# Gathered expert rows transposed by DMA instead of TensorE, their weights gathered in two parts, in an attention and two-layer expert kernel

## The chip, the cores and the metric

One core of one Trainium2 chip runs the whole program. The metric is device time in microseconds (us) of one execution. Of the kernel before, three runs were timed: 1859.72, 1863.57 and 1864.79, median 1863.57 us.

## What is computed

A strided/local attention (4 batches, 8 heads, 576 positions, head size 64) gives 2304 tokens of 512 numbers. A first expert layer (8 experts, hidden size 1024) applies all experts to all tokens with Sinkhorn weights. The second expert layer, which the change touches, gives each token to one expert, 288 tokens to each:

```python
def _moe2_ref(x, w_gate, w1, w2):
    N, D = x.shape
    E = w_gate.shape[1]
    cap = N // E
    logits = x @ w_gate
    flat = logits.flatten()
    order = np.argsort(-flat)
    ...
    for idx in order:
        tok, e = (int(idx) // E, int(idx) % E)
        if assigned[tok] >= 0 or counts[e] >= cap:
            continue
        assigned[tok] = e
        counts[e] += 1
    ...
    for e in range(E):
        mask = assigned == e
        h = np.maximum(x[mask] @ w1[e], 0.0)
        out[mask] = h @ w2[e]
```

## The kernel before

Attention and the first expert layer take the first 1600 us and are not touched. They leave each token's row in DRAM as `xd`: 512 high halves and 512 low halves in fp16, and a scale, 2052 bytes in all. The weights of the second layer lie in DRAM as four tensors `wd[0..3]` (high and low halves of the first and of the second matrix), 1 MB for each expert and tensor.

The second layer is done in eight phases, one for each expert, in an order that the routing finds while the phases run (`ffn`, L1532; `ph` is the phase's number). A phase has a first matrix (8 blocks `f`, 12 matmuls each, L1549) and a second one (4 blocks `d`, 24 matmuls each, L1579). The results are turned back by TensorE (`pty`, L1522) and stored row by row (L1525) in the next phase's first matrix.

What the next phase needs comes in three ways:

- The routing (`route`, `place`) names the next expert (`wis`) and its tokens (`places`). It is a chain between TensorE and VectorE: compare (L1211), count (`pcnt`, L1217), select (L1219), `pany` (L1223) and so on, and at last `pidx` (L1394) and the list of row numbers (L1400).
- `load_w2` gathers the four weight tensors from DRAM, as soon as `wis` is known, into one of three sets of buffers (`w3`).
- `ffn_g` gathers the 288 rows as three tiles `g0` to `g2` of 96 rows each, as soon as `places` is known; this is at block `d` = 1. `ffn_x` then turns one tile: 8 transposes on TensorE into one bank `ptg` (L1469), a copy by ScalarE into `xg` (L1470), and the rows' scales `osc` on VectorE (L1471). It is called for the three tiles in the middle of `d` = 2, at the start of `d` = 3 and in the middle of `d` = 3. The first matrix of the next phase reads all 288 columns of `xg` in each matmul, so it needs all three tiles.

Phase 0 gets its `xg` in another way (`ffn_x0`), which is not changed; so there are seven turns from a phase to the next, 21 tiles in all.

The order of TensorE's work is the order in which this code is written: `drive` draws units of `ffn` and steps of the routing in turn. On the other engines a scheduler sets the order in each engine's stream, by when it expects each instruction to be ready. GpSimd (POOL) issues all the gathers and row stores, SyncE (SP) issues the plain DMAs and has none left after the last `xd` store (L1073).

Of the kernel before, what the change touches and what calls it, by code (L numbers as in the profile page):

```python
# [10 lines left out]
F16 = mybir.dt.float16  # L11
BF16 = mybir.dt.bfloat16
I32 = mybir.dt.int32
AF = mybir.ActivationFunctionType
# [4 lines left out]
N, DM, E, F = 2304, 512, 8, 1024  # L19
CAP = N // E  # L20
WIN = 32
DC = DM // 128
# [233 lines left out]
class Kernel:  # L256
# [21 lines left out]
    def bank(self, name, tag="bank"):  # L278
        tag = tag if tag in self.banks else "l1"
        return self.psum.tile([128, 512], F32, name=name, tag=tag, bufs=self.banks[tag])  # L280
# [1154 lines left out]
                t = next(routes, None)  # L1435
                self.wait = 1e9 if t is None else self.wait + t

    def load_w2(self, ph):
        for k in range(4):
            self.nc.gpsimd.indirect_dma_start(out=self.w3[ph % 3][k].rearrange("p a b -> p (a b)"), out_offset=None,  # L1440
                                              in_=self.wd[k],
                                              in_offset=bass.IndirectOffsetOnAxis(ap=self.wis[ph][:, :1], axis=0))
# [16 lines left out]
    def ffn_x(self, ph, s):  # L1459

        nc = self.nc
        M = 96
        if s == 0:
            self.fx[ph] = (self.fp.tile([128, 2 * DC, CAP], F16, name="xg"), self.fp.tile([96, 3], F32, name="osc"))
        gs = self.gs[ph]
        xg, osc = self.fx[ph]
        pt = self.bank("ptg", "l2").bitcast(F16)[:, 0:2 * DC * M].rearrange("p (k m) -> p k m", m=M)
        for k in range(2 * DC):
            nc.tensor.transpose(pt[:, k], gs[s][:, k * 128:k * 128 + 128], self.identh[:M, :M])  # L1469
        nc.scalar.activation(xg[:, :, s * M:s * M + M], pt, AF.Copy)  # L1470
        nc.vector.tensor_tensor(osc[:, s:s + 1], gs[s][:, 2 * DM:].bitcast(F32), self.places[ph][1][:M], op=OP.mult)  # L1471

    def ffn_x0(self):
# [58 lines left out]
    def ffn(self, routes):  # L1532

        nc, fp = self.nc, self.fp
        bank = lambda: self.bank("mm", "l1")[:, :CAP]
        for ph in range(E):
            w = self.w3[ph % 3]
            if ph + 1 < E:
                loaded = False
            xg = self.fx[ph][0]  # L1540
            hh = fp.tile([128, FC, CAP], F16, name="h2h")
            hl = fp.tile([128, FC, CAP], F16, name="h2l")
            for f in range(FC):
                ps = bank()
                fs = slice(f * 128, f * 128 + 128)
                k = 0
                for d in range(DC):
                    for l, r in ((w[0], d), (w[0], DC + d), (w[1], d)):
                        nc.tensor.matmul(ps, l[:, d, fs], xg[:, r], start=k == 0, stop=k == 3 * DC - 1)  # L1549
                        k += 1  # L1550
                    if d == 1:
                        yield
                r = fp.tile([128, CAP], F32, name="h2", bufs=5)
                nc.scalar.activation(r, ps, AF.Relu)  # L1554
                nc.scalar.activation(hh[:, f], r, AF.Copy)
                nc.vector.tensor_tensor(hl[:, f], r, hh[:, f], op=OP.subtract)
                yield
                if ph and 0 < f < 4:
                    self.ffn_y(ph - 1, f - 1)
                if ph + 1 < E and not loaded:  # L1560
                    if f == 5:
                        self.until_has(self.wis, ph + 1, routes)
                    if len(self.wis) > ph + 1:
                        self.load_w2(ph + 1)
                        loaded = True
            yt = self.fy[ph] = fp.tile([128, DC, CAP], F32, name="yt")
            for d in range(DC):
                if ph + 1 < E and d == 1:
                    self.until_has(self.places, ph + 1, routes)
                    if ph + 1 not in self.gs:  # L1570
                        self.ffn_g(ph + 1)
                if ph + 1 < E and d == 3:
                    self.ffn_x(ph + 1, 1)
                ps = bank()
                dsl = slice(d * 128, d * 128 + 128)
                k = 0
                for f in range(FC):
                    for l, r in ((w[2], hh), (w[3], hh), (w[2], hl)):
                        nc.tensor.matmul(ps, l[:, f, dsl], r[:, f], start=k == 0, stop=k == 3 * FC - 1)  # L1579
                        k += 1  # L1580
                    if f % 2 and f < FC - 1:
                        if ph + 1 < E and (d, f) in ((2, 5), (3, 3)):
                            self.ffn_x(ph + 1, 2 * d - 4)
                        if ph + 1 == len(self.places) < min(len(self.wis), E):
                            self.spare()
                        yield
                nc.scalar.activation(yt[:, d], ps, AF.Copy)
                yield
        for s in range(3):
            self.ffn_y(E - 1, s)  # L1590
# [239 lines left out]
```

## Time and profile before

| | |
|---|---|
| median of 3 runs | 1863.57 us |
| profiled execution, its own time | 1860.97 us |
| span of its instructions | 1859.2 us |
| TensorE (PE) busy | 1791.8 us, 96% |
| VectorE (DVE) busy | 1192.3 us, 64% |
| ScalarE (ACT) busy | 858.3 us, 46% |
| GpSimd (POOL) busy | 474.0 us, 25% |
| mean DMA rate | 124 GB/s |
| mean granted TensorE clock | 0.985 of full |

The span runs from the first to the last instruction; the rest of the profiled execution's own time lies around it. PE rows are matmuls, PEld rows weight loads that run beside them. A time in brackets behind a row is how long the engine sat idle before it and what it then waited for. Times in the rows of a timeline are from the start of the span; a matmul's row ends some 0.2 us after the next one starts, so what a piece of PE work takes is read from start to start.

### The profile page before, as it was taken

The numbers are of one execution on the slowest core, as the hardware profiler recorded it, in microseconds if no ns is written. First come the engines' busy times: TensorE is split into PE (matmuls) and PEld (weight loads), VectorE is DVE, ScalarE is ACT, GpSimd is POOL, SyncE is SP. The second block draws the span as 40 slices with busy tenths as digits, with TensorE's granted clock in tenths as the row PEclk, the third lists the DMA queues.
The fourth block names the chain that finished last, engine by engine and source line by source line (L and its number), as shares of the span: only waits on it lengthen the run. The fifth ranks groups of instructions, "written<-read, shape, count | busy, mean of one in ns | idle before, by whom it ended". The sixth has DMA issues, their size and how long they took to land. (4 is left out here: it accounts for less than half of the span.)

```text
span 1859.2 us, 31850 instructions
## 1 busy us (share of the span) xinstructions
PE 1791.8 (96%) x12296; PEld 1058.9 (57%) x12296; DVE 1192.3 (64%) x3081; ACT 858.3 (46%) x1956; POOL 474.0 (25%) x469
## 2 busy tenths in 40 slices
PE   7889998999999999999999999999999999899997
PEld 5757765555555545554555555555555444687786
DVE  6645456678766676667476575674673788767640
ACT  6545542476667757873324511565121110234343
POOL 2121203145434544433101300322000001323241
PEclk8889999999999999999999999999999999999999
DMA  7121021245655757653322323063011001445460
GB/s 249 57 71 41 26 80 46 80 176 193 205 197 200 238 180 251 222 171 144 125 70 78 107 76 113 35 229 134 35 46 51 24 23 62 161 154 179 172 233 26
DMA packets 77420, 230.48 MB, mean 124 GB/s; under 512 B 8580, under 2 KB 13260, under 8 KB 68660
## 3 DMA queue, kind: packets, MB, share of 16 engines
q1 hardware_dynamic: 69588, 185.44, 28.7%
q0 software_dynamic: 7680, 43.01, 6.4%
q8 instruction: 96, 1.57, 0.3%
q14 instruction: 56, 0.46, 0.1%
HBM read 165.47 MB, written 62.94 MB: 123 GB/s over the span
## 5 line engine op out<-in xcount | busy, mean ns | idle before, releaser
L978 PEld LDWEIGHTS <-w1s 128*128 128x128 f16 x3024 | 295.2, 98 | 203.2 <-issue 6.4
L1034 PE MATMUL l<-w2h,hh 128*128 128x512 f16 x864 | 327.7, 379 | 0.0
L1034 PE MATMUL l<-w2h,hl 128*128 128x512 f16 x864 | 327.7, 379 | 0.0
L1034 PE MATMUL l<-w2l,hh 128*128 128x512 f16 x864 | 327.7, 379 | 0.0
L586 POOL TENSOR_TENSOR m2l<-raw,m2h 128x512 f16<-128x512 f32 x184 | 214.6, 1168 | 335.2 <-ACT raw L585 286.7
L978 PE MATMUL l<-sx,w1s 128*128 128x384 f16 x1728 | 287.9, 326 | 4.5 <-ACT vV L993 2.0
L1034 PEld LDWEIGHTS <-hh 128*128 128x128 f16 x1728 | 168.4, 98 | 199.7
L978 PE MATMUL l<-xh,w1s 128*128 128x384 f16 x864 | 219.7, 326 | 0.7 <-ACT junk L1091 0.7
L936 DVE TENSOR_REDUCE wmx<-raw 128x1 f32<-128x512 f32 x240 | 152.4, 676 | 59.8 <-DMA raw<-in_moe_w_dram 54.6
L745 DVE SCALAR_TENSOR_TENSOR acc<-l,pe,acc 128x512 f32<-128x512 f32 x126 | 94.3, 748 | 139.8 <-PE l L1034 125.0
L892 POOL TENSOR_TENSOR raw<-raw 128x256 f32<-128x256 f32 x96 | 90.2, 944 | 291.1 <-DVE w1s L582 283.5
L584 ACT ACTIVATE m2h<-raw,wscale 128x512 f16<-128x512 f32 x184 | 130.9, 712 | 63.3 <-DVE iw L948 17.1
L993 ACT ACTIVATE vV<-l 128x384 f32<-128x384 f32 x144 | 67.9, 486 | 188.9 <-PE l L978 185.2
L698 ACT ACTIVATE hh<-l 128x256 f16<-128x256 f32 (+1 forms) x112 | 49.7, 447 | 223.9 <-PE l L695 223.6
L1034 PEld LDWEIGHTS <-hl 128*128 128x128 f16 x864 | 84.5, 98 | 102.0
L978 PE MATMUL l<-xl,w1s 128*128 128x384 f16 x432 | 141.0, 326 | 0.0
L585 ACT ACTIVATE raw<-raw,wscale 128x512 f32<-128x512 f32 x184 | 132.8, 722 | 6.0
L713 PE MATMUL l<-w2h,hh 128*128 128x512 f16 x288 | 109.8, 381 | 0.0
L713 PE MATMUL l<-w2h,hl 128*128 128x512 f16 x288 | 109.7, 381 | 0.0
L713 PE MATMUL l<-w2l,hh 128*128 128x512 f16 x288 | 109.7, 381 | 0.0
L1079 DVE SCALAR_TENSOR_TENSOR junk<-acc,raw 128x512 f32<-128x512 f32 x144 | 99.0, 688 | 2.0 <-DMA raw<-gt 0.2
L582 DVE SCALAR_TENSOR_TENSOR w1s<-raw,wscale,w1s 128x512 f16<-128x512 f32 x96 | 83.0, 904 | 20.2 <-ACT w1s L581 20.2
(360 smaller groups left out, 3081.2 us busy)
## 6 DMA issues: line engine op xcount, KB each, us to landing
raw<-in_moe_w_dram SPq DMA_DIRECT2D x120, 512.0 KB, 5.2
sx<-sd SPq DMA_DIRECT2D x15, 1536.0 KB, 6.8
wd<-m2h SPq DMA_DIRECT2D x64, 256.0 KB, 4.7
wd<-m2l SPq DMA_DIRECT2D x64, 256.0 KB, 3.3
kq<-in_qk_dram SPq DMA_DIRECT2D x16, 592.0 KB, 3.9
sd<-sx SPq DMA_DIRECT2D x3, 1536.0 KB, 5.1
acc<-in_moe_w_dram SPq DMA_DIRECT2D x2, 2048.0 KB, 14.0
vl<-in_vl_dram SPq DMA_DIRECT2D x4, 768.0 KB, 6.2
```

Source lines behind the costliest of these rows:

```text
L582: nc.vector.scalar_tensor_tensor(lo, raw, s, hi, op0=OP.mult, op1=OP.subtract)
L584: nc.scalar.activation(hi, raw, AF.Copy, scale=s)
L585: nc.scalar.activation(raw, raw, AF.Copy, scale=s)
L586: nc.gpsimd.tensor_tensor(lo, raw, hi, op=OP.subtract)
L713: nc.tensor.matmul(ps, l[:, f, js], r[:, f], start=k == 0, stop=k == 3 * FC - 1)
L745: self.last = [nc.vector.scalar_tensor_tensor(a, ps, pe[:, c:c + 1], a, op0=OP.mult, op1=OP.add).ins]
L892: nc.gpsimd.tensor_tensor(o, x, y, op=OP.subtract)
L936: nc.vector.tensor_reduce(mx[:, 2 * q + k:2 * q + k + 1], part(q)[:, k * 512:k * 512 + 512], axis=AX.X, op=OP.max, apply_absolute_value=True)
L978: self.nc.tensor.matmul(ps, self.w1s[:, fs, x, k, d], a[y][:, d], start=first and m == 0, stop=m == 5, skip_group_check=not first)
L993: copy = lambda o, i: nc.scalar.activation(o, i, AF.Copy)
L1034: nc.tensor.matmul(ps, l[:, f, js], r[:, f], start=k == 0, stop=k == 3 * FC - 1)
L1079: self.nc.vector.scalar_tensor_tensor(junk, self.acc[:, c], 1.0, self.wgb[:, e], op0=OP.mult, op1=OP.mult, accum_out=self.lg[:, c, e:e + 1])
```

## The change

The transposes and the copy of `ffn_x` become one transposing DMA issued by SyncE, from the gathered tile straight into `xg`. All three calls stand right behind the gather, at block `d` = 1. The weights' gather is split: tensors 0 and 1 are asked for where all four were, tensors 2 and 3 behind the row gather at `d` = 1. The line numbers after L1466 shift by 3 to 4.

```diff
-    def load_w2(self, ph):
-        for k in range(4):
+    def load_w2(self, ph, ks=range(4)):
+        for k in ks:
...
-        pt = self.bank("ptg", "l2").bitcast(F16)[:, 0:2 * DC * M].rearrange("p (k m) -> p k m", m=M)
-        for k in range(2 * DC):
-            nc.tensor.transpose(pt[:, k], gs[s][:, k * 128:k * 128 + 128], self.identh[:M, :M])
-        nc.scalar.activation(xg[:, :, s * M:s * M + M], pt, AF.Copy)
+        nc.sync.dma_start(out=xg[:, :, s * M:s * M + M], in_=gs[s][:, 0:2 * DM], transpose=True)
         nc.vector.tensor_tensor(osc[:, s:s + 1], gs[s][:, 2 * DM:].bitcast(F32), self.places[ph][1][:M], op=OP.mult)
...
-                        self.load_w2(ph + 1)
+                        self.load_w2(ph + 1, (0, 1))
                         loaded = True
...
                     if ph + 1 not in self.gs:
                         self.ffn_g(ph + 1)
-                if ph + 1 < E and d == 3:
-                    self.ffn_x(ph + 1, 1)
+                        for n in range(3):
+                            self.ffn_x(ph + 1, n)
+                    self.load_w2(ph + 1, (2, 3))
...
-                        if ph + 1 < E and (d, f) in ((2, 5), (3, 3)):
-                            self.ffn_x(ph + 1, 2 * d - 4)
```

Where the instructions stand after it, at three places of the turn from phase 1 to phase 2. On TensorE before, the first tile's transposes (tile `g_16733` is `g0`) stand between the second matrix and a count of the routing:

```order
18568 L1579 LDWEIGHTS acc
18569 L1579 MATMUL mm<-h2l,acc 128x288
18570 L1469 LDWEIGHTS g_16733
18571 L1469 MATMUL ptg<-identh,g_16733 128x96
...
18586 L1217 LDWEIGHTS sx
18587 L1217 MATMUL pcnt<-w1s,sx 128x40
```

They are gone, as are the 20 other blocks of eight; the matmuls before and the count behind now follow each other. On SyncE the stream ended with the `xd` stores; now 21 transposing DMAs follow, those of phase 1 and of phase 2 first:

```order
353 L1467 DMA_TRANSPOSE xg<-g_16189 128x8x96
354 L1467 DMA_TRANSPOSE xg<-g_16191 128x8x96
355 L1467 DMA_TRANSPOSE xg<-g_16193 128x8x96
356 L1467 DMA_TRANSPOSE xg<-g_16704 128x8x96
357 L1467 DMA_TRANSPOSE xg<-g_16706 128x8x96
358 L1467 DMA_TRANSPOSE xg<-g_16708 128x8x96
```

Nothing stands between or behind them on this engine. On GpSimd, before, in the first matrix of phase 1 (the weights for phase 2 are `wd_73` to `wd_76`, the row stores of phase 0 are `out_dram`):

```order
136 L1525 DMA out_dram<-y,raw_3216 2304x512
137 L1440 DMA w1s<-wd_73,raw_3216 128x4096
138 L1525 DMA out_dram<-y,raw_3216 2304x512
139 L1440 DMA w1s<-wd_74,raw_3216 128x4096
140 L1440 DMA w2h<-wd_75,raw_3216 128x4096
141 L1440 DMA w2l<-wd_76,raw_3216 128x4096
142 L1525 DMA out_dram<-y,raw_3216 2304x512
143 L1454 DMA g_16733<-xd,raw_3216 96x1026
```

and of the change:

```order
136 L1522 DMA out_dram<-y,raw_3216 2304x512
137 L1440 DMA w1s<-wd_73,raw_3216 128x4096
138 L1522 DMA out_dram<-y,raw_3216 2304x512
139 L1440 DMA w1s<-wd_74,raw_3216 128x4096
140 L1522 DMA out_dram<-y,raw_3216 2304x512
141 L1440 DMA w2h<-wd_75,raw_3216 128x4096
142 L1440 DMA w2l<-wd_76,raw_3216 128x4096
143 L1454 DMA g_16704<-xd,raw_3216 96x1026
```

The second two weight tensors move behind one row store, and still stand ahead of the rows' gather. In the other turns it is one to three stores.

## Rows read from the trace of the kernel before

**Rows 1.** The page: busy time, share of the span, instructions.
```profile
PE 1791.8 (96%) x12296; PEld 1058.9 (57%) x12296; DVE 1192.3 (64%) x3081; ACT 858.3 (46%) x1956; POOL 474.0 (25%) x469
```

**Rows 2.** Busy time by stretch: phase 1, from its first matmul to that of phase 2.
```profile
core 0: us, PE busy (x) PEld busy (x) DVE busy (x) ACT busy (x) POOL busy (x), PEclk, DMA share, GB/s
1640.70:1671.20 30.50, 30.21 (x367) 25.30 (x365) 22.86 (x103) 12.57 (x26) 9.78 (x10) 1.00 0.48 178
```

**Rows 3.** Groups of instructions, 1606 to 1860: what the change removes (busy, mean ns).
```profile
L1469 PE MATMUL ptg<-identh,g 96*128 96x96 f16 x168 | 10.6, 206 | 0.0
L1470 ACT ACTIVATE xg<-ptg 128x768 f16<-128x768 f16 x21 | 17.0, 810 | 30.8 <-PE ptg L1469 23.9 <-PE pany L1223 6.8
```

**Rows 4.** Timeline of PE, one block of eight transposes and its neighbours.
```profile
1665.37 0.29 PE L1579 MATMUL mm<-h2l,acc 128*128 128x288 f16 x1
1665.49 0.51 PE L1469 MATMUL ptg<-identh,g 96*128 96x96 f16 x8
1665.84 0.62 PE L1217 MATMUL pcnt<-w1s,sx 128*128 128x40 bf16 x18
```

**Rows 5.** Timeline, turn to phase 2: row numbers ready, last gather, last scale, `pany`.
```profile
1660.30 0.14 DVE L1400 CAST raw<-raw 96x1 int32<-96x1 f32 x1
...
1663.29 0.92 POOL L1454 DMA_INDIRECT g<-xd,raw  x1 [0.30 <-DVE w1s L1219]
...
1666.59 0.16 DVE L1471 TENSOR_TENSOR osc<-g,raw 96x1 f32<-96x1 f32 x1 [0.99 <-DMA g<-xd,raw]
...
1667.03 0.18 PE L1223 MATMUL pany<-w1s,first 128*128 128x40 bf16 x1
```

**Rows 6.** The three scales of the turns to phases 1 to 6: first and last start.
```profile
L1471 DVE TENSOR_TENSOR osc<-g,raw x3: 145/147/150, 1633.2 to 1635.6; 96x1 f32<-96x1 f32 x3
...
L1471 DVE TENSOR_TENSOR osc<-g,raw x3: 148/155/156, 1664.0 to 1666.6; 96x1 f32<-96x1 f32 x3
...
L1471 DVE TENSOR_TENSOR osc<-g,raw x3: 145/146/155, 1696.6 to 1697.8; 96x1 f32<-96x1 f32 x3
...
L1471 DVE TENSOR_TENSOR osc<-g,raw x3: 154/155/156, 1727.2 to 1729.0; 96x1 f32<-96x1 f32 x3
...
L1471 DVE TENSOR_TENSOR osc<-g,raw x3: 154/155/156, 1759.0 to 1760.0; 96x1 f32<-96x1 f32 x3
...
L1471 DVE TENSOR_TENSOR osc<-g,raw x3: 155/155/226, 1788.6 to 1790.1; 96x1 f32<-96x1 f32 x3
```

**Rows 7.** Timeline of PE: first matmuls of phases 1 to 7.
```profile
1640.69 1.51 PE L1549 MATMUL mm<-xg,acc 128*128 128x288 f16 x11
...
1671.16 0.90 PE L1549 MATMUL mm<-xg,w1s 128*128 128x288 f16 x6
...
1704.44 0.90 PE L1549 MATMUL mm<-xg,xh 128*128 128x288 f16 x6
...
1735.78 1.39 PE L1549 MATMUL mm<-xg,acc 128*128 128x288 f16 x10
...
1767.55 0.90 PE L1549 MATMUL mm<-xg,w1s 128*128 128x288 f16 x6
...
1795.77 1.51 PE L1549 MATMUL mm<-xg,xh 128*128 128x288 f16 x11
...
1821.63 3.10 PE L1549 MATMUL mm<-xg,acc 128*128 128x288 f16 x24
```

**Rows 8.** SyncE's `xd` stores of 256.5 KB, 1595 to 1610: issue (ns), time to landing.
```profile
L1073 SPq DMA_DIRECT2D xd<-w1s x2: 319/319/319, 1600.3 to 1604.2; - x2
...
DMA to landing us min/median/max: 2.6/2.6/2.6
```

**Rows 9.** The rows' gathers `g` (21 of 192 KB), 1606 to 1860: time to landing.
```profile
DMA to landing us min/median/max: 3.1/4.2/10.2
```

**Rows 10.** PE's waits, 1595 to 1860: us in total, times, longest.
```profile
PE pcnt L1217 <- DVE w1s L1211: 3.6, 4, 2.4
PE pany L1223 <- DVE w1s L1219: 3.3, 4, 1.6
```

## Prediction

> **What bounds the kernel now.** I read the page first, then the busy time by stretch, then the timeline of one turn between phases, then TensorE's waits. The page shows TensorE busy for 96% of the span and no other engine above 64% [rows 1]. The stretch of phase 1 says the same of the place that the change touches: 30.21 of 30.50 us busy at full clock, with the DMA engines half idle [rows 2]. So in the eight phases a microsecond taken from TensorE is a microsecond of the kernel, unless TensorE then waits for something else. The reader is to see two possible somethings. One is the routing's chain through VectorE: TensorE already waits for it 8 times, 6.9 us in all [rows 10]. The other is new: the first matmul of a phase needs all three transposed tiles, and these will come by DMA.
>
> **What is removed.** 168 transposes on TensorE [rows 3], 21 blocks of eight. The group's mean of 206 ns is not the price, since the instructions overlap; from start to start a block takes 1665.84 - 1665.49 = 0.35 us [rows 4]. 21 x 0.35 = 7.35 us of TensorE. The 21 copies on ScalarE, 17.0 us [rows 3], are worth nothing: ScalarE is busy 12.57 of 30.5 us in the phase [rows 2], and no wait of TensorE names it beside the two for VectorE that matter.
>
> **What of the 7.35 us is lost at once.** A block that stands between two steps of the routing also gave VectorE time. In the turn to phase 2 VectorE sat in the last `osc` until the rows had landed at 1666.59, and `pany` on TensorE followed at 1667.03 [rows 5]. That chain doesn't move with the block ahead of it, so this block's 0.35 us turns into a wait. I count two such blocks in all, 0.7 us. The bounds are none and the 15 blocks of the turns to phases 1 to 5, where the routing still runs: 5.25 us. I take a value near the low end because TensorE has only 8 waits of this kind in some 60 steps of the routing.
>
> **What is added.** 21 DMAs of 96 x 1024 fp16 numbers, 192 KB each. On SyncE they stand alone, behind its last `xd` store at 1604.2 [rows 8], so nothing is queued behind a transfer that waits for its rows but the next transfer. They occupy no compute engine. What matters is when the third one lands against when TensorE wants it. The row numbers, the gathers and the scales keep their places, so the rows land as before. The start of the last `osc` bounds this landing: in the turn to phase 2 it waited for just that [rows 5]. Without the three blocks TensorE wants `xg` 1.05 us sooner than the first matmul of the next phase shows [rows 7]. That leaves, from the third landing to the need:
>
> - to phase 1: 1640.69 - 1.05 - 1635.6 = 4.0 us
> - to phase 2: 1671.16 - 1.05 - 1666.6 = 3.5 us
> - to phase 3: 5.6; to phase 4: 5.7; to phase 5: 6.5; to phase 6: 4.6 us [rows 6, 7]
>
> In the turn to phase 7 the first matmul stands at 1821.63 and the routing has long ended; I count no wait there.
>
> **The price of a transposing DMA** is in no row. The nearest below is SyncE's store of 256.5 KB, issued in 0.32 us and landed in 2.6 us [rows 8]. The nearest above is the slowest gather of the same 192 KB tiles, 10.2 us; their median is 4.2 us [rows 9]. I take 2.6 us: same queue, like size, and in most turns the weights' traffic is over by then (DMA share 0.48 over the phase [rows 2]), while the 10.2 us belongs to a gather that queued behind weights. A transfer is issued before the one ahead has landed, as the stores are, so the third lands 2.6 us after its rows, inside the 3.5 us of the tightest turn. The wait is then 0.
>
> Here the Trainium skill speaks with two voices. "Advanced Engine Details and Errata", section "X-Bar Transpose (TRN2)", says that transposing DMAs are as fast as regular ones; by it the sum stays as it is. "VectorE: DVE Perf Modes", section "The three transpose paths", speaks against the change: it gives 390 ns to TensorE and 1309 ns to the DMA for one 128x128 block. Counted so, as an estimate, a tile of eight blocks costs 10.5 us and the six turns would wait about 149 us. No row here transposes by DMA; of TensorE's price the rows show far less, 0.35 us for eight blocks of 96 rows [rows 4].
>
> **The weights in two parts.** No work is added: 4 gathers before, 4 after. On GpSimd's stream the second two move behind one to three row stores and still stand ahead of the rows' gather, so the rows queue behind the same bytes. Each store or gather occupies GpSimd for about a microsecond [rows 5], so the second two start 1 to 4 us later. They are first read in the second matrix of the next phase, more than 15 us on: nothing. What the words say of it, two parts, hardly happens in the order of the instructions.
>
> **The sum.** -7.35 + 0.7 + 0 = -6.6 us. Against the profiled execution's own time, 1860.97, that is 1854.4. That execution lies 2.6 us under the median of the runs, so against the median 1863.57 it is 1857.0 us, 0.35% less. A measurement of this kernel can tell about 0.3%, 5.6 us, from no change; the forecast lies just beyond.
>
> **Rivals.**
>
> 1. *The transfers run one after another, at 2.6 us each.* Then the third ends 7.8 us after the first rows landed. From there to the need the six turns leave 6.4, 6.1, 6.8, 7.5, 7.5 and 6.1 us [rows 6, 7], 40.4 in all; the waits add up to 18 x 2.6 - 40.4 = 6.4 us and eat the gain: 1863.4. For it: three transfers of one queue within 1 to 3 us. Against it: the stores' 0.32 us of issue.
>
> 2. *The other side: a transposing transfer is slow, and TensorE stands at the first matmul of each phase.* One mechanism, in the six turns: transfers in turn at T each make waits of 18 T - 40.4 us. It decides from T = 2.61, where the waits equal the gain of 6.6. At 4.2 us, the median of the gathers [rows 9], the waits are 35.2 and the time is 1863.57 + 35.2 - 6.6 = 1892.2. For it: a transposing write comes in smaller pieces than any store shown, and the turn to phase 2 has only 3.5 us of room. Against it: in these turns the DMA engines have little else to do.
>
> 3. *The same at the upper end, 10.2 us a transfer* [rows 9]: 183.6 - 40.4 = 143.2 us of waits, 2000.2 us, leaving out the turn to phase 7. It is nearly what the rule of the skill's "VectorE: DVE Perf Modes" on the three transpose paths would give. Against it: such a gather shared the engines with 4 MB of weights, and that is so in the last turns alone.
>
> 4. *The routing becomes the bound.* All 15 blocks of the first five turns turn into waits for VectorE: -7.35 + 5.25 = -2.1, 1861.5. For it: VectorE is busy 22.86 of 30.5 us in the phase [rows 2]. Against it: the few waits [rows 10].
>
> **How the numbers follow.** Forecast (third transfer in time): 0.48, of which 0.33 end over 0.3% faster and 0.15 within, since 6.6 us lies so near to 5.6. Rival 1: 0.14 (0.02 faster, 0.08 same, 0.04 slower). Rival 2: 0.22, slower. Rival 3: 0.08, slower. Rival 4: 0.08 (0.01 faster, 0.07 same). Together: faster 0.36, same 0.30, slower 0.34. The predicted time is the forecast's, 1857.0. The range begins at 1855.0, where no block is lost and the runs fall a little lower, and reaches to 1892, rival 2 at the gathers' median. Outside lie rival 3, the upper part of rival 2 (0.08) and a little at the low end (0.04). The forecast's own range is 1855 to 1860.
>
> **What would show it.** Right: no group `ptg`; TensorE busy some 10 us less by the page's count; the transposing DMAs landing about 2.6 us after issue; the first matmul of each phase without a wait; the turn to phase 2 about 1 us shorter in the busy time by stretch. Rival 1 or 2: the wait view names the first L1546 matmuls behind the DMA of `xg`, the longest in the turns to phases 1, 2 and 6, and landings of the three tiles a constant step apart. Rival 4: more and longer waits at `pcnt` and `pany`. What would make the prediction wrong is above all the price of the transfer, the one number that no row carries.

## The result, and the profile after

The change takes **1886.3 us** (median of 4 runs, 1883.77 to 1891.35), the kernel before 1864.18 us (median of 4 runs beside it, 1859.72 to 1867.39). The ratio is 1.0126, 95% interval 1.0107 to 1.0144: 22 us slower by the medians and some 23.5 us by the ratio. The forecast was 6.6 us faster. The profiled execution of the change took 1883.77 us with a span of 1882.1 us, against 1860.97 and 1859.2.

The page's busy line, which answers to [rows 1]: 168 transposes fewer on TensorE and 21 copies fewer on ScalarE, as the diff says, but TensorE's busy time has not fallen: it reads 1798.1 us against 1791.8.

```profile
PE 1798.1 (96%) x12128; PEld 1057.6 (56%) x12128; DVE 1191.7 (63%) x3081; ACT 841.8 (45%) x1935; POOL 473.9 (25%) x469
```

The first matmuls of the phases, from PE's timeline (answering to [rows 7]; brackets at the end of a row hold the idle time ahead and its releaser):

```profile
1645.23 0.65 PE L1546 MATMUL mm<-xg,acc 128*128 128x288 f16 x4
...
1675.09 0.78 PE L1546 MATMUL mm<-xg,w1s 128*128 128x288 f16 x5
...
1706.34 0.65 PE L1546 MATMUL mm<-xg,xh 128*128 128x288 f16 x4
...
1739.54 0.65 PE L1546 MATMUL mm<-xg,acc 128*128 128x288 f16 x4
...
1770.41 0.65 PE L1546 MATMUL mm<-xg,w1s 128*128 128x288 f16 x4
...
1817.96 4.30 PE L1546 MATMUL mm<-xg,xh 128*128 128x288 f16 x20 [15.30 <-DMA acc<-wd,raw]
...
1844.47 0.78 PE L1546 MATMUL mm<-xg,acc 128*128 128x288 f16 x5
```

In six of the seven turns TensorE doesn't wait at the phase's first matmul. In the turn to phase 6 it stands for 15.30 us. That is most of what this execution loses: the phases are 17.0 us longer in sum (from the first matmul of phase 0, 1612.83, to the end: 269.3 us against 252.3). The other 5.9 us of the profile's difference lie ahead of phase 0, which starts at 1612.83 here and at 1606.94 before. Another profiled execution of the kernel before, taken later, starts phase 0 at 1613.38, so this part is taken as scatter between executions.

The stretches of phase 1 and phase 5 (answering to [rows 2]; same columns) show the good and the bad turn:

```profile
1645.23:1675.09 29.86, 29.45 (x343) 24.30 (x340) 22.82 (x103) 10.18 (x23) 9.91 (x10) 1.00 0.61 201
1770.42:1817.96 47.54, 29.13 (x246) 23.08 (x244) 15.28 (x83) 10.60 (x24) 16.50 (x17) 0.86 0.96 231
```

Phase 1 went from 30.47 to 29.86 us. Phase 5, with the turn to phase 6 at its end, went from 28.22 to 47.54. Of before, the same stretch reads:

```profile
1767.54:1795.76 28.22, 28.22 (x270) 23.52 (x268) 15.32 (x83) 12.47 (x26) 15.54 (x16) 1.00 0.82 311
```

DMA share 0.82 and 311 GB/s: this is the one phase in which the weights of two phases are in flight, and it is not like phase 1 (0.48, 178 GB/s).

The group of the transposing DMAs (issue in ns min/median/max, first and last start; time from issue to landing in us), for the turn to phase 5 and then for the turns to phases 6 and 7 together:

```profile
L1467 SPq DMA_TRANSPOSE xg<-g x3: 1213/1287/1288, 1762.0 to 1764.6; - x3
...
DMA to landing us min/median/max: 2.9/2.9/2.9
...
L1467 SPq DMA_TRANSPOSE xg<-g x6: 1258/3856/6182, 1791.6 to 1815.0; - x6
...
DMA to landing us min/median/max: 10.6/14.7/18.9
```

The same instruction on the same number of bytes takes 2.9 us in one turn and 10.6 to 18.9 in these two. The trace has three of the six landings: 18.9 us is the second tile of phase 6; 14.7 and 10.6 are the first and second of phase 7, whose tiles were issued from 1804.0 on and landed without making TensorE wait. In the turns to phases 1 to 5 the landings are 2.9 to 4.4 us. In the slow turns the issue itself is slow too, 5.9 us for the second tile of phase 6 and up to 6.18 for those of phase 7, and the next tile queues behind it on SyncE. The third tile of phase 6 was issued only at 1798.8, some 7 us after the first; its landing is not in the trace.

What else was under way, from POOL's timeline (GpSimd's gathers: `xl` holds the second matrix of phase 6, `acc` the weights of phase 7):

```profile
1780.72 0.97 POOL L1440 DMA_INDIRECT xl<-wd,raw  x1 [0.30 <-issue]
1782.60 0.97 POOL L1454 DMA_INDIRECT g<-xd,raw  x1 [0.91 <-DVE raw L1400]
...
1785.11 0.92 POOL L1454 DMA_INDIRECT g<-xd,raw  x1 [0.30 <-DVE h2l L1553]
1786.33 0.95 POOL L1440 DMA_INDIRECT xl<-wd,raw  x1 [0.30 <-issue]
1787.59 0.95 POOL L1440 DMA_INDIRECT acc<-wd,raw  x1 [0.30 <-issue]
1788.85 0.94 POOL L1440 DMA_INDIRECT acc<-wd,raw  x1 [0.30 <-issue]
1795.12 0.93 POOL L1454 DMA_INDIRECT g<-xd,raw  x1 [5.34 <-DVE raw L1400]
...
1798.81 0.95 POOL L1440 DMA_INDIRECT acc<-wd,raw  x1 [0.30 <-issue]
1800.07 0.95 POOL L1440 DMA_INDIRECT acc<-wd,raw  x1 [0.30 <-issue]
```

So the last weights of phase 6 (1786.33) stand behind that phase's rows. In the kernel before they stood ahead of them:

```profile
1774.69 1.01 POOL L1440 DMA_INDIRECT xl<-wd,raw  x1 [0.31 <-issue]
...
1779.97 0.94 POOL L1454 DMA_INDIRECT g<-xd,raw  x1 [0.30 <-DVE h2l L1556]
```

The text ahead of the result says of every turn that the second two tensors stay ahead of the rows. That holds in the turns to phases 1 to 5 and not in the last two. In phase 5 the routing also ends, and phase 7's expert is known before the phase is over. Together 5 MB of weights, one part of phase 6 and four of phase 7, and the rows of phase 7 are asked for between 1786.3 and 1800.1, around phase 6's transposes (issued at 1791.6, 1792.9 and 1798.8). The busy time by stretch over it:

```profile
1795.00:1800.00 5.00, 5.00 (x32) 3.59 (x31) 0.00 (x0) 0.65 (x2) 3.72 (x4) 0.75 1.17 258
1800.00:1805.00 5.00, 2.66 (x22) 1.88 (x20) 0.00 (x0) 0.58 (x2) 0.95 (x1) 1.00 1.61 189
1805.00:1810.00 5.00, 0.00 (x0) 0.00 (x0) 0.00 (x0) 0.00 (x0) 0.00 (x0) 0.78 1.18 67
1810.00:1815.00 5.00, 0.00 (x0) 0.00 (x0) 0.00 (x0) 0.00 (x0) 0.00 (x0) 0.50 0.76 240
1815.00:1820.00 5.00, 2.04 (x9) 1.31 (x10) 0.00 (x0) 0.00 (x0) 0.00 (x0) 0.50 0.96 244
```

From 1805 to 1810 the DMA engines count as fully busy (1.18) and move 67 GB/s, a quarter of what they moved ten microseconds earlier. No engine computes. The granted clock falls to 0.50, the lower of its two levels (1.2 GHz), and phase 6 starts at that clock.

The wait view puts the 15.3 us down to `acc<-wd`, the DMA that came last. But `acc` holds weights of phase 7, and the first matrix of phase 6 reads `xg` and `xh`. The two `xh` gathers were asked for at 1773.6 and 1774.9 and landed within 9.9 us, long before TensorE ran out of work at 1802.7. That leaves `xg`, or a wait for `acc` that the code doesn't ask for; the experiments had to tell.

### The profile page after: what moved, and what is told of

It reads as the page before. It is cut to its first block, busy times and chain, and to the rows that moved or that the text cites. A ratio compares the mean times of both kernels' runs of the same rounds, so it can differ in the third digit from the quotient of the medians.

```text
span 1882.1 us, 31551 instructions
## 1 busy us (share of the span) xinstructions
PE 1798.1 (96%) x12128; PEld 1057.6 (56%) x12128; DVE 1191.7 (63%) x3081; ACT 841.8 (45%) x1935; POOL 473.9 (25%) x469
## 6 DMA issues: line engine op xcount, KB each, us to landing
acc<-in_moe_w_dram SPq DMA_DIRECT2D x2, 2048.0 KB, 12.2
```

## The experiments

**Theories.** T1: the transposes of the turn to phase 6 stand behind weight gathers in flight beside them. T2: they are limited by their own queue and issue, whatever else moves. T3: TensorE waits for phase 6's weights. T4: the weights' split into two parts is the cause. After the first group there was a fifth, T5: the split has a cost of its own in phases 3 and 5, through VectorE. The runs came from four chips. On the first the kernel before takes 1864 to 1866 us, on the three others 1892 to 1894; ratios are always to the kernel before on the same chip in the same group of runs.

### First group: take one suspect away (first chip, before 1864.91 us)

**Phase 7's weights held back.** The four gathers take an index that depends on phase 6's first block.

```diff
-  in_offset=bass.IndirectOffsetOnAxis(ap=self.wis[ph][:, :1], axis=0))
+  in_offset=bass.IndirectOffsetOnAxis(ap=(self.w7i if ph == E - 1 else self.wis[ph])[:, :1], axis=0))
...
+  if ph + 1 == E - 1 and f == 0:
+      self.until_has(self.wis, ph + 1, routes)
+      w7f = self.rt.tile([128, 1], F32, name="w7f", bufs=1)
+      nc.vector.tensor_copy(w7f, self.wis[ph + 1])
+      self.w7i = self.rt.tile([128, 1], I32, name="w7i", bufs=1)
+      nc.vector.tensor_scalar(self.w7i, r[:, 0:1], 0.0, w7f, op0=OP.mult, op1=OP.add)
```

> The changed kernel, but phase 7's four weight gathers are held until phase 6's first block of the second-layer hidden rows is out, so they can't share the DMA engines with the three transposes of the turn to phase 6. All transposes stay on DMA. Theory T1 (the transposes of that turn stand behind weight gathers in flight, and that alone makes the 15.6 us gap): the gap ahead of phase 6 falls under 3 us and the time to 1860 to 1872 us (the weights of phase 7 then come later and may cost some us in its first matrix). Rival T2 (the transposes' own queue or issue is slow there whatever else moves): the gap stays over 10 us and the time over 1880. Rival T3 (TensorE waits for phase 6's weights): phase 6's own weights move as before, so the gap stays, over 10 us.

Measured: 1868.02 us, ratio 1.0012 (0.9999 to 1.0025). The transposes of the turns to phases 6 and 7, and the first matmul of phase 6, now without a wait:

```profile
L1467 SPq DMA_TRANSPOSE xg<-g x6: 1213/1300/1698, 1792.8 to 1802.5; - x6
...
DMA to landing us min/median/max: 3.7/4.0/4.6
```

```profile
1803.72 1.02 PE L1546 MATMUL mm<-xg,xh 128*128 128x288 f16 x7
```

Landings of 3.7 to 4.6 us in place of 10.6 to 18.9, with the queue, the tiles and the order on SyncE unchanged. T2 falls. Phase 6's own weights were asked for as in the change, the last part behind the rows, so T3 falls, as their landing in the change's trace said already. But the time is back only to that of before: the saved 7.35 us are not there.

**TensorE transposes again in the turns to phases 6 and 7**, the five others by DMA, split kept.

```diff
+    def ffn_xp(self, ph, s):
...
-                        for n in range(3):
+                        for n in range(3 if ph + 1 < 6 else 0):
...
+                if ph + 1 < E and d == 3 and not (ph + 1 < 6):
+                    self.ffn_xp(ph + 1, 1)
...
+                        if ph + 1 < E and (d, f) in ((2, 5), (3, 3)) and not (ph + 1 < 6):
+                            self.ffn_xp(ph + 1, 2 * d - 4)
```

(`ffn_xp` is `ffn_x` of the kernel before.)

> The changed kernel, but the turns to phases 6 and 7 transpose on TensorE as the kernel before; the turns to phases 1 to 5 by DMA; weights in two parts everywhere. T1: no gap ahead of phase 6, five turns keep about 1 us of gain each at most, two pay 1.05 us as before: 1857 to 1862 us, the same as before or up to 0.4% faster. T3 (phase 6's weights are late): the gap of about 15 us stays, and the time is over 1876 us. T4 (the split itself delays the rows): a gap stays, now as a wait of the first transposes on the rows.

Measured: 1869.08 us, ratio 1.0021 (1.0008 to 1.0035), no gap in that turn. This also answers whether TensorE stands for `acc`. Here too the four gathers of phase 7 are in flight. The last two are asked for at 1796.2 and 1797.4, and the last lands 9.1 us later, at 1806.5; phase 6 starts at 1801.01 without a wait:

```profile
L1440 POOL DMA_INDIRECT acc<-wd,raw x2: 948/950/952, 1796.2 to 1797.4; - x2
...
DMA to landing us min/median/max: 7.9/8.5/9.1
```

```profile
1801.01 0.65 PE L1560 MATMUL mm<-xg,xh 128*128 128x288 f16 x4
```

So it was `xg`. T1 had the gap right and the time wrong: slower than before, where 15 blocks of 0.35 us should have been won.

**The split undone**, DMA everywhere.

```diff
-                        self.load_w2(ph + 1, (0, 1))
+                        self.load_w2(ph + 1)
...
-                    self.load_w2(ph + 1, (2, 3))
```

> The changed kernel with the weights' split undone: all four gathers asked for at the old place; transposes on DMA everywhere. T1: the weights of phases 6 and 7 are still in flight during the transposes, so the gap ahead of phase 6 stays, 8 to 25 us, and the time is 1875 to 1895. T4 (the split puts weight gathers behind the rows and so beside the transposes, and is the cause): the gap falls under 3 us and the time to about 1861.

Measured: 1868.18 us, ratio 1.0012 (0.9999 to 1.0024). The gap ahead of phase 6 is 8.2 us, as T1 says, and PE's waits here name the tile itself:

```profile
PE mm L1546 <- DMA xg<-g: 8.2, 1, 8.2
```

T1's time was a miss: 1868 instead of 1875 and more. T4 falls as the only cause, since a gap stays, but the split is part of it. Undoing it alone, with phase 7's weights still in flight, takes the ratio from 1.0126 to 1.0012, as much as holding those weights does with the split kept. The trace shows what moved: phase 6's last weights are asked for at 1773.90, ahead of the rows (1779.18 on), and phase 7's rows only at 1811.04, behind the start of phase 6. So only the four gathers of phase 7's weights lie beside the transposes. Which of the two moves halved the gap was not separated. Phases 1 to 4 are 30.47, 30.48, 30.54 and 30.76 us long here, together 4.6 us less than the 126.85 of the kernel before [rows 7]; phase 1 alone is no shorter.

**The split alone**, TensorE transposes everywhere.

```diff
-                        self.load_w2(ph + 1)
+                        self.load_w2(ph + 1, (0, 1))
...
+                    self.load_w2(ph + 1, (2, 3))
```

> The kernel before with the weights' split alone; all transposes on TensorE. T1: within 0.3% of the kernel before, 1859 to 1868 us, no gap in any turn. T4 (the split costs time by itself): a wait of 3 to 15 us at the first transposes or the first matrix of phase 6 or 7, 1868 to 1881 us.

Measured: 1871.71 us, ratio 1.0028 (1.0013 to 1.0042). That is still inside T1's 0.3%, but the interval leaves out no change, and T1 has no place for it. T4 fits the size but not the place, since no gap stands at phase 6. Phase 3, before and then with the split alone:

```profile
1704.44:1735.78 31.34, 30.34 (x371) 25.34 (x367) 22.10 (x101) 12.28 (x26) 11.76 (x10) 1.00 0.49 174
```

```profile
1713.86:1748.18 34.32, 31.84 (x371) 26.22 (x367) 22.16 (x101) 12.35 (x26) 11.75 (x10) 0.95 0.48 159
```

The chain in it: the last of the weights was asked for 10.2 us after the phase's start before, and 14.6 us after it with the split; the rows at 18.7 us in both. So more of the weights is still in flight when the rows are asked for. Landings of the three row gathers of that turn, before and with the split alone:

```profile
DMA to landing us min/median/max: 3.1/3.1/3.1
```

```profile
DMA to landing us min/median/max: 4.6/5.4/6.3
```

VectorE waits for those rows in the scale, and TensorE's `pany`, a step of the routing, waits for VectorE. The two rows with the split alone (its line for the scale is L1482), and for comparison `pany` of before:

```profile
1738.89 0.16 DVE L1482 TENSOR_TENSOR osc<-g,raw 96x1 f32<-96x1 f32 x1 [2.35 <-DMA g<-xd,raw]
```

```profile
1740.24 0.18 PE L1223 MATMUL pany<-w1s,first 128*128 128x40 bf16 x1 [2.30 <-DVE w1s L1219]
```

```profile
1729.36 0.18 PE L1223 MATMUL pany<-w1s,first 128*128 128x40 bf16 x1 [0.83 <-DVE w1s L1219]
```

After the pause of 2.30 us the granted clock is at its lower level; in phase 3 of the kernel before, with the pause of 0.83 us, it stays at 1.00. Busy time by stretch behind the longer pause:

```profile
1741.00:1743.00 2.00, 2.00 (x16) 1.44 (x15) 0.84 (x2) 0.78 (x1) 0.00 (x0) 0.50 0.00 0
1743.00:1745.00 2.00, 2.00 (x34) 1.69 (x33) 0.26 (x1) 0.85 (x3) 0.00 (x0) 0.74 0.00 0
```

So 1.5 us more of waiting becomes 3.0 us more of phase 3 here. It is no rule: in phase 2 the kernel before pauses for 2.42 us, and the granted clock is 1.00 over the whole phase:

```profile
1697.37 0.82 PE L1217 MATMUL pcnt<-w1s,sx 128*128 128x40 bf16 x18 [2.42 <-DVE w1s L1211]
```

```profile
1671.16:1704.44 33.28, 30.80 (x383) 25.78 (x381) 22.93 (x102) 12.76 (x27) 9.97 (x10) 1.00 0.47 163
```

Why the one pause brings the lower clock and the other doesn't stays open. Phases 1 and 5 are longer as well in this execution, 34.36 us instead of 30.47 and 31.43 instead of 28.22: by the run's wait view a transpose waits 1.3 us for the rows in the one, and `pidx` 1.3 us for VectorE in the other, each with a granted clock of 0.95 over the phase. This profiled execution is the slowest of its ten (1876.84 us), so its phases overstate the cost. From this came T5.

### Second group: add traffic, take both costs away (a second chip, before 1891.93 us)

**Weights gathered twice** in the turns to phases 1 to 5: tensors 2 and 3 of the next phase once more, with an index that depends on the first tile of rows. It asks for the same data again.

```diff
+                    if ph + 1 < 6:
+                        wf = self.rt.tile([128, 1], F32, name="wf")
+                        nc.vector.tensor_copy(wf, self.wis[ph + 1])
...
+                        nc.vector.tensor_scalar(wx[:96], self.gs[ph + 1][0][:, 2 * DM:].bitcast(F32), 0.0, wf[:96], op0=OP.mult, op1=OP.add)
+                        self.load_w2(ph + 1, (2, 3), wx)
```

> The changed kernel, and in the turns to phases 1 to 5 the second two weight tensors are gathered a second time as soon as the first tile of rows has landed, 2 MB of traffic beside the three transposes. T1 (weight gathers in flight slow the transposes): landings of the 15 transposes in these turns rise from 2.9 to 4.4 us to over 5, up to some 15, and gaps of 1 to 10 us stand ahead of phases 1 to 5; the time is over 1895 us. T2 (only the queue of the transposes matters): landings in these turns stay at 3 to 4.5 us, no new gap, 1880 to 1892 us.

Measured: 1945.75 us, ratio 1.0282 (1.0253 to 1.0311). Waits of 6.8, 5.2, 2.9, 9.3 and 5.4 us now stand ahead of phases 1 to 5, where there were none, and 26.6 ahead of phase 6. PE's waits for the tile, phases 0 to 5:

```profile
PE mm L1546 <- DMA xg<-g: 29.6, 5, 9.3
```

Five waits for the transposed tile, 29.6 us. That the rows were late instead can be ruled out in the turn to phase 2, where the three transfers were issued at the usual pace once their rows were there, by 1684.7, and phase 2 started at 1694.99:

```profile
1680.42 4.29 SPq L1467 DMA_TRANSPOSE xg<-g  x3
```

```profile
1694.99 1.36 PE L1546 MATMUL mm<-xg,w1s 128*128 128x288 f16 x5 [5.22 <-DMA xg<-g]
```

Together with the first run this shows T1 from both sides: taking the gathers away removes the wait, putting gathers beside the transposes makes one. The trace gives no landing times for these 15 transfers, so that part of the expectation stays open.

**No split, TensorE in the turn to phase 6 alone**, the other six turns by DMA (the two diffs above, with `ph + 1 != 6` as the condition).

> Weights gathered all at once as before; the turn to phase 6 transposed on TensorE as before; the other six turns by DMA. T1: no gap, 18 blocks of 0.35 us saved, some given to the routing: 1858 to 1861 us where the kernel before stands at 1865, 0.2 to 0.4% less. T5 (the split, by making the rows land about a microsecond later, is what lengthened phases 3 and 5 by 1.5 to 3 us with VectorE in the scales, TensorE behind it and then a half clock): phases 3 and 5 are 30.5 and 27.5 to 28.5 us long, at granted clock 1.00, as in the run without the split. Rival (the freed time is all given to the routing's waits): 1864 to 1866, the same as before.

Measured: 1886.05 us, ratio 0.9973 (0.9958 to 0.9987), no gap in any turn. The times expected were those of the first chip; by the ratio T1 holds. T5's expected lengths can't be read here, since all phases 1 to 5 are 34 to 36 us long on this chip. This runs on below.

**No split, phase 7's weights held**, DMA in all seven turns.

> All seven turns by DMA, weights all at once as before, but phase 7's four gathers held until phase 6's first block is out. T1 and T5 together: no gap ahead of phase 6 (under 1 us), phases 3 and 5 at full clock, 1857 to 1862 us. If phase 6's own weights are enough traffic to slow the transposes, a gap of 2 to 8 us ahead of phase 6 and 1862 to 1868 us.

Measured: 1887.10 us, ratio 0.9975 (0.9964 to 0.9986), no gap. By the ratio it is as T1 and T5 together say.

**Scales later**: the run with TensorE in the turn to phase 6, and the scales worked out in the next phase's first block.

```diff
-        nc.vector.tensor_tensor(osc[:, s:s + 1], gs[s][:, 2 * DM:].bitcast(F32), self.places[ph][1][:M], op=OP.mult)
...
+                if ph and f == 0:
+                    pl = self.rt.tile([96, 1], F32, name="pl")
+                    nc.vector.tensor_scalar(pl, r[:96, 0:1], 0.0, self.places[ph][1][:96], op0=OP.mult, op1=OP.add)
+                    for s in range(3):
+                        nc.vector.tensor_tensor(self.fx[ph][1][:, s:s + 1], self.gs[ph][s][:, 2 * DM:].bitcast(F32), pl, op=OP.mult)
```

> The run with TensorE in the turn to phase 6 and the weights at once, and in addition the rows' scales on VectorE are worked out in the first block of the next phase (their factor made to depend on that block's result), so VectorE never stands waiting for gathered rows ahead of a routing step. If VectorE in the scales is what TensorE's waits at the routing's counts come from: the waits at pcnt and pany fall from 5.6 us in all to under 3 us, and the time falls by another 2 to 4 us, to 1855 to 1859. Rival (the routing's own chain is late whatever VectorE does before): the waits and the time stay within 1 us.

Measured: 1887.25 us, ratio 0.9971 (0.9959 to 0.9983), the same as the run beside it. TensorE's waits at `pcnt` and `pany` are 8.5 us in its trace against 10.0 beside it, and not under 3. The time is as the rival said: with the rows in time there is nothing more to gain at the scales. With the split kept, where T5 puts the loss, later scales were not tried, so T5's way through VectorE rests on the traces alone.

### Third group: the steps one after the other on one chip (first chip, before 1864.12 us)

The kernel before for its trace, the change again, the first run (weights held) again, and the same without the split.

> The kernel before, for its trace on the chip that the next three runs use. On the chip of the second group of runs all kernels, the one before too, took 27 us more than on the first. If this run is on that chip: phases 1 to 5 are about 34 to 35 us long instead of 30.5 to 31.8, with a pause of ScalarE of 4 to 5 us in the first matrix of each, and about 1892 us; else the phases as before and about 1865 us.

> The change again, beside the two steps that take its costs away one after the other. T1 and T5: ratio to the kernel before 1.010 to 1.015, with a gap of 12 to 18 us ahead of phase 6. A chip on which the weights land later in general may make the gap longer.

> The change with phase 7's weights held back (as the first run). T1: ratio 0.999 to 1.003, no gap ahead of phase 6, phases 3 and 5 longer than in the run without the split.

> The same with the weights gathered all at once. T5: the ratio falls by 0.002 to 0.005 more against the run with the split on the same chip, to 0.995 to 0.999. Rival (the split costs nothing; the lower ratio of the second group was the other chip's): the same ratio as the run with the split, within 0.001.

| | median us | ratio | 95% interval | wait ahead of phase 6 |
|---|---|---|---|---|
| before, own run | 1865.72 | 1.0010 | 0.9995 to 1.0026 | none |
| the change | 1890.53 | 1.0133 | 1.0116 to 1.0150 | 24.1 us |
| weights held | 1866.88 | 1.0020 | 1.0009 to 1.0032 | none |
| held, no split | 1862.59 | 0.9988 | 0.9974 to 1.0001 | 2.0 us |

Holding the weights is worth 0.0113, some 21 us. Undoing the split as well is worth another 0.0032, some 6 us by the ratio and 4.3 by the medians, so T5's size is as expected and the rival falls. In this pair of traces the split's cost stands in phase 5 (33.17 against 29.35 us) and hardly in phase 3 (31.53 against 30.73, both at a clock of 1.00). The order of the two steps matters: undone first (1.0126 to 1.0012), the split is worth 0.0114, and holding the weights then adds some 0.0024. The wait of the change was longer than expected (24.1 instead of 12 to 18 us).

That leaves a question: without both costs the kernel was only 0.12% faster here, and the interval includes no change, where the forecast had 0.35%. Its trace shows a wait in the turn to phase 6 after all, and phase 0 is longer than in the kernel before's trace, 34.62 us at a clock of 0.86 against 33.74 at 0.93:

```profile
PE mm L1546 <- DMA xg<-g: 2.0, 1, 2.0
```

### Fourth to sixth group: what is left of the gain

No split, TensorE in the turn to phase 6, again, and once more with the later scales:

> The run with weights at once and TensorE in the turn to phase 6 alone, again, now on whichever chip comes, beside the next. The run with held weights and no split kept a wait of 2.0 us for a transposed tile ahead of phase 6 and half clock behind it. If that is all that kept it at 0.12% under the kernel before, this one, which has no transfer in that turn, stands at a ratio of 0.9965 to 0.998 (four to six of the 6.3 us that 18 blocks are worth). Rival (most of the saved TensorE time turns into other waits): 0.998 to 1.000, with phases 1 to 4 shorter than before by less than 0.5 us each.

> The same with the rows' scales worked out in the next phase, so that VectorE doesn't wait for gathered rows. On the second group's chip it made no difference, 0.9971 against 0.9973. Theory that VectorE in the scales still costs TensorE 2 to 4 us where the routing is close: 0.001 to 0.002 less than the run beside it. Rival (no more to gain there): within 0.0007.

Both came on a third chip, as slow as the second: 1887.06 us, ratio 0.9974 (0.9961 to 0.9986), and 1889.43, ratio 0.9984 (0.9968 to 1.0001). The later scales gain nothing, again.

Then beside a trace of the kernel before:

> The kernel before, for a trace beside the next run on the same chip. If it is the chip on which all kernels take 27 us more: phases 1 to 5 of 34 to 36 us with a pause of ScalarE of about 5 us in each, so that the extra time is the chip's and not the kernels'; else phases as in the rows shown.

> Weights at once, TensorE in the turn to phase 6 alone. The saved time stays saved: ratio 0.9965 to 0.998; on the first chip 1858.5 to 1861, phases 1 to 4 shorter than before by 0.6 to 1.4 us each, phase 6 by 1.0. Rival: 0.998 to 1.000 on the first chip.

The second chip again: before 1893.17 us, ratio 0.9997 (0.9984 to 1.0010); the other 1887.28, ratio 0.9970 (0.9955 to 0.9985). From the first matmul of phase 0 to that of phase 7 the kernel before takes 240.98 us there (1613.56 to 1854.54) and the other 235.41 (1611.03 to 1846.44): 5.6 us of the 6.3 that 18 blocks are worth. That is one pair; the same stretch of this version takes 232.1 to 235.4 us in its four traces. The extra 27 us of this chip are in the kernel before too, 25.9 of them in phases 1 to 5. Its ScalarE pauses for 3.7 to 5.9 us in the first matrix of each of these phases, and never for over 3 us in the trace of the third group. A row of ACT's timeline:

```profile
1663.86 0.41 ACT L1554 ACTIVATE h<-mm 128x288 f32<-128x288 f32 x1 [4.93 <-PE mm L1549]
```

What ends this pause was not tried.

And last both versions side by side:

> Weights at once, TensorE in the turn to phase 6 alone, beside the version with held weights in the same chip's runs. On the first chip: phases 1 to 4 as in the other runs without the split (30.4 to 31.2 us), no gap, phase 6 24.8 us; ratio 0.996 to 0.998. Rival: 0.9985 or more, then the saved time is lost on that chip in something that both versions share.

> Held weights, no split, all seven turns by DMA. On the first chip: a wait of about 2 us ahead of phase 6 again, ratio 0.9975 to 1.000 and 0.001 to 0.002 more than the run beside it.

A fourth chip, as slow as the second and third: 1884.09 us, ratio 0.9962 (0.9948 to 0.9976), and 1888.86, ratio 0.9971 (0.9959 to 0.9984). The first beats the kernel before in all four measurements (0.9962 to 0.9974, on three chips) and, by the ratios, the change by far. How large its gain is on the first chip stays open, since no run of it came there. There the other version gained 0.0012, against 0.0025 and 0.0029 on two of the slower chips. The intervals of the two versions overlap.

## Why the prediction was wrong

**The value of a block was right.** 0.35 us of TensorE for eight transposes. The cleanest place is phase 6, with the turn to phase 7 and no routing. Its whole length at full clock, in the kernel before and with the weights held (both of the third group):

```profile
1801.84:1827.70 25.86, 25.86 (x230) 21.14 (x228) 4.04 (x11) 12.47 (x26) 3.91 (x4) 1.00 0.27 86
```

```profile
1800.78:1825.61 24.83, 24.83 (x206) 20.14 (x204) 4.18 (x12) 10.20 (x23) 7.07 (x7) 1.00 0.59 204
```

25.86 - 24.83 = 1.03 us for three blocks, where the sum had 1.05.

**The blocks lost to the routing: not contradicted.** The forecast lost two, 0.7 us. Without the split, phases 1 to 4 take 122.25 us (the run with the split undone) against 126.50 (the kernel before of the third group): 4.25 us for 12 blocks worth 4.2. With held weights and no split it is 3.26. These are single executions, and the kernel before itself reads 126.85 in another.

**The price of a transposing DMA: near in five turns, and the failing step in the sixth.** The prediction took 2.6 us in every turn, because "in most turns the weights' traffic is over by then (DMA share 0.48 over the phase [rows 2]), while the 10.2 us belongs to a gather that queued behind weights". In the turns to phases 1 to 5 the landings are 2.9 to 4.4 us and nothing waits, though an issue takes 1.2 to 1.7 us and not the 0.32 of [rows 8]. That a transfer is issued before the one ahead has landed came true (1.3 us apart, 2.9 us each), but [rows 8] didn't show it: its two stores start 3.9 us apart and land in 2.6. In the turn to phase 6 the transfer is itself the one that queues with weights. The one landing that the trace has there is 18.9 us, beyond the upper bound of 10.2, against a room of 4.6 us. The wrong reading was to let the DMA share of phase 1 speak for all turns; phase 5 has 0.82 and 311 GB/s. That the last turns are the ones with weights in flight stood in the prediction, as the argument against rival 3. It was used to dismiss the high price and not to place it.

**Where the lost time goes.** Some 21 us are this wait with the half clock behind it. It is no fixed amount: 15.3 us of waiting in one execution, 24.1 in another. 8.2 us of waiting are left without the split, none with phase 7's weights held, and none with TensorE's transposes in that turn. Most of the loss is neither part's own: the new transfers without the split stand at 1.0012 and the split without the new transfers at 1.0028, but the two together at 1.0126.

**The weights in two parts: the second term that failed. It was nothing, and it is some 5 to 6 us by itself** (ratio 1.0028 alone; 0.0032 between the two held runs) **and some 21 us beside the new transfers** (1.0126 against 1.0012 with the split undone). The prediction said that the second two tensors "still stand ahead of the rows' gather, so the rows queue behind the same bytes". In the turns to phases 1 to 5 the bytes are the same, but in phase 3 they are asked for 4.4 us later, while the rows are asked for at the same point. The rows land 2.3 us later by the median, VectorE and then TensorE wait for them, and in most of the traces with the split the clock is lower behind that wait. In the turn to phase 6 one of the two stands behind the rows, and so beside the transposes.

**The rivals.** Rival 1 (one after another) didn't come: three transfers of 2.9 us are issued 1.3 us apart in the turn to phase 5. Rival 2 gave 1892.2 us, near the measured 1886.3, which therefore lies inside the stated range. That is luck: rival 2 named the turn to phase 6 among the places to look, but its mechanism, 4.2 us in each of six turns, isn't what happened, since five turns waited for nothing. Rival 3's 10.2 us came, and more, in one turn. Rival 4 (routing) appeared only through the split.

Of the two rules of the Trainium skill that the prediction set beside the trace: "VectorE: DVE Perf Modes", section "The three transpose paths", gave 10.5 us for a tile, as an estimate. The trace does not agree where a transfer runs without weights beside it (2.9 us for eight blocks). "Advanced Engine Details and Errata", section "X-Bar Transpose (TRN2)", says as fast as regular DMAs. That is near the trace in the same turns (2.9 us for 192 KB against 2.6 for the stores of 256.5 KB in [rows 8]), and the 18.9 us of the turn to phase 6 have no place in it.

## What to carry to other kernels

Cost a transfer turn by turn with the traffic of that turn, above all where a pipeline drains and two stages' loads come together; the quiet phase's price is no price for the busy one. A gather that is asked for later "because it isn't needed yet" lands on whatever is asked for next; look at who that is and who waits for it. Where one turn of several is bad for a new path, keep the old one there: six turns by DMA and one by TensorE, with the weights asked for at once, beats both kernels by the ratios, on the three chips where it ran. And where a change has two parts, try each part alone too: here each cost under 0.3% by itself and the two together 1.3%.

## What was not expected of the hardware

- A transposing DMA and weight gathers in flight slow each other. In the change, from 1770 to 1818 the transposes' queue (q1) moved 0.79 MB and the gathers' queue (q0) 10.16 MB; the share is the time of their packets on 16 engines:

```profile
q0 software_dynamic: 1728, 10.16, 68.1%
q1 hardware_dynamic: 3222, 0.79, 26.8%
```

Per byte the transposes' packets took five times as much engine time as the gathers'. Their packets are small, about 245 bytes each (0.79 MB / 3222). From 1762 to 1768, in the turn to phase 5, without weight gathers beside them:

```profile
q1 hardware_dynamic: 2400, 0.59, 52.6%
```

Worked out from these rows, a MB of transposes took some 86 us of one engine's time there and some 260 in the crowded stretch, three times as much with packets of the same size. The gathers suffer too: those of phase 7's weights landed in 12.2 to 17.9 us in the change and in 7.9 to 11.3 where TensorE did that turn's transposes. What inside the engines makes it so was not tried.

- A pause of TensorE can cost as much again at half clock behind it (phase 3 with the split alone: 1.5 us more of waiting, 3.0 us more of phase), or nothing: after 2.30 us the clock was 0.50, after 2.42 us in phase 2 of the kernel before it was 1.00.
- Four chips fell into two kinds on the same kernel: one took 1864 to 1866 us, three took 1892 to 1894, with pauses of ScalarE in the one trace of the kernel before that was taken on them. The ratios between versions stayed within 0.0017 of each other across chips.
